# Expert weights split once and reloaded as parts, and a planner that orders the readers of a PSUM bank

## The chip, the cores and the metric

One of the cores of a Trainium2 chip runs the whole program. The metric is the device time of one execution in microseconds (us). Below, PE is TensorE, PEld its weight loads, DVE is VectorE, ACT is ScalarE, POOL is GpSimd, and SP is SyncE, whose queue issues most DMAs.

## The reference

Three layers follow each other, in fp32, on 8 batches of 3072 tokens of width 256:

```python
attn = np.maximum(z @ z.T / S, 0.0) ** 2       # per batch
x = u * (attn @ v)
# expert layer: tokens with x @ w_skip > 0 go to their argmax expert of 8
h = np.maximum(xc[mask] @ w1[e], 0.0)
y[mask] = gate_w[mask, None] * (h @ w2[e])      # x[do_compute] += y
# rational layer, on every token
h = x @ w_in
P = a[0] + a[1] * h + a[2] * h2 + a[3] * h3
Q = 1.0 + np.abs(b[0]) * np.abs(h) + np.abs(b[1]) * h2
out = (P / (Q + 1e-06)) @ w_out
```

## The kernel before

Every fp32 operand of a large matrix product is kept as two parts, hi (a rounded copy) and lo (the operand less hi), and a product takes three matmuls (hi hi, hi lo, lo hi) in PE's fp32r format. Splitting an operand of 128x512 costs one copy and one subtraction on ACT, DVE or POOL.

**Work units.** Attention goes in 1152 ticks (a 512 x 256 block of scores: matmuls, relu and square on ACT, split on ACT or DVE, product with V). The expert and the rational layer go in 1024 units of 256 tokens by 256 hidden columns; each unit has 12 matmuls into a PSUM bank h (L1030), elementwise work, and 12 matmuls into the accumulator bank accM (L1041), of which there is one. An expert unit needs ACT's relu (L1166, hi) and DVE's subtraction (L1169, lo). A rational unit, number t, needs, in order of its names in `plan_unit`: abs (ACT, L1174, reads h), p1 (ACT, L1175, reads h), q0 (ACT, POOL or DVE, L1181 or L1179), q1 (DVE or POOL, the L394 multiply mq<-mq,mu), p2 (DVE, L1187, reads h), p3 (DVE, L1188), ln and ex (ACT, L1189 and L1190), gh (DVE, L1191), v (DVE, L1192), w (DVE, L1194, the last reader of h, which frees the bank) and gl (POOL or DVE, the L394 multiply mgl<-mq,mu).

**Stages.** The batches form five groups of 1, 2, 2, 2 and 1. A group's tokens go through attention, are scattered to their experts, then through the expert units, then the rational units; attention ticks of the next group are mixed in between. In the profile: ticks alone to 366 us; the first group's 32 expert units to 464; its rational units with ticks to 1300; expert units of the second group to 1535, its rational units with ticks to 2720; the same for the third group (2720 to 2945 to 4085) and the fourth (4085 to 4310 to 5020, the last ticks in it). From 5020 to 5370 comes a **mixed stage** without attention: 56 rational units of group four and the 32 expert units of group five. The **last stage** (5370 to the end) is the 96 rational units of group five.

**Weights.** An expert has four chunks; a chunk is a 128x512 piece of w1 and one of w2. `plan_w1` loads a chunk's two pieces in fp32 (two DMAs of 256 KB on SP's queue into the ring wr), makes hi by two copies and lo by two subtractions, into a tile W of 128x2048 (a ring of eight). It does so for each of the four groups with an expert stage of their own and, with other buffers (Wr, Wv), for group five: 160 times for 32 different chunks. The rational layer's weights are converted and split once, at the start, stored in DRAM as wsc, and loaded as parts by POOL's queue (L973).

**What sets the order.** All instructions are placed by a list scheduler in the kernel itself (`Flow`). Each operation has a due time, shifted by a table of numbers (`PAR`), an estimate of its length on each engine that could do it, what it waits for, and buffers that it takes and frees. `Flow.run` fixes which engine does it and the order on each engine. Waits in the built program are put in by the framework from the tiles and banks that an instruction reads and writes, in that order; the engines run their queues strictly in order.

## Time and profile before

| | before |
|---|---|
| median of 3 runs (lowest to highest) | 5769.25 us (5768.03 to 5769.51) |
| profiled execution: time, span | 5767.14 us, 5765.4 us |
| granted TensorE clock, mean | 0.994 |
| busy: PE, DVE, ACT, POOL | 5498.1, 4701.9, 4315.3, 3309.7 us |
| DMA: moved, mean | 335.30 MB, 58 GB/s |

Busy time is the sum over the span, and it hides that stages differ: the table of stages in the rows below gives, for each stage, its length and each engine's busy time in it. PE's busy time less the stage's length is what PE waited there. The list of waits names, for one engine in one stretch, whose instruction ended each wait.

### The profile page before, as it was taken

Reading aid. Unit: us, or ns where it says so; the run is one execution under the profiler, and the core shown is the slowest. Engines: PE = TensorE matmul, PEld = TensorE weight load, DVE = VectorE, ACT = ScalarE, POOL = GpSimd, SP = SyncE. Lnnn points to the kernel's source line nnn. Section 1 sums busy time; section 2 is a strip of 40 time slices with the busy share of each in tenths; the row PEclk is TensorE's granted clock in tenths of the full one; section 3 lists DMA queues with packets and bytes.
Section 4 is the critical chain, followed back from the end, with each engine's and each line's share of the span. In section 5 each row is a group of like instructions: output and inputs, shape, how many; then the busy total and the mean of one; then the engine's idle time right before and its main releaser. Section 6 shows DMA issues by size and latency. Waiting matters only on the chain.

```text
span 5765.4 us, 119268 instructions
## 1 busy us (share of the span) xinstructions
PE 5498.1 (95%) x45285; PEld 5417.3 (94%) x45285; DVE 4701.9 (82%) x7546; ACT 4315.3 (75%) x7907; POOL 3309.7 (57%) x4614
## 2 busy tenths in 40 slices
PE   9999999999999999999999999999999999988887
PEld 8999999999999999999999999999999999887776
DVE  6766777776588888888568899889759999988999
ACT  7877787885488888888458888888638888755776
POOL 3443444445565665666455675567556666655677
PEclk9999999999999999999999999999999999999999
DMA  4353111023400100011330010001241000122000
GB/s 134 105 167 116 30 59 32 31 62 94 151 27 30 53 31 31 28 52 45 105 127 24 27 59 27 29 25 54 72 143 50 24 22 24 37 81 65 19 19 14
DMA packets 261771, 335.30 MB, mean 58 GB/s; under 512 B 31102, under 2 KB 211817, under 8 KB 256066
## 3 DMA queue, kind: packets, MB, share of 16 engines
q1 hardware_dynamic: 233922, 259.87, 14.6%
q0 software_dynamic: 27264, 67.71, 3.4%
q8 instruction: 358, 5.87, 0.4%
q14 instruction: 227, 1.86, 0.1%
HBM read 224.54 MB, written 119.54 MB: 60 GB/s over the span
## 4 chain that ended last, share of the span: by engine, by line
PE 59%; DVE 19%; ACT 8%; issue 6%; POOL 6%; DMA 1%; SPq 0%; DVEq 0%; POOLq 0%; ACTq 0%
PE accA L672 20%; PE h L1030 15%; PE accM L1041 14%; DVE mq L1192 4%; PE S L649 4%; PE S L650 3%; DVE mp L1187 3%; DVE mgh L1191 3%; DVE mq L1194 3%; ACT mu L1174 2%; POOL mq L394 2%; DVE h L1188 2%; ACT mp L1175 2%; DVE al L664 1%; ACT mu L1189 1%
## 5 line engine op out<-in xcount | busy, mean ns | idle before, releaser
L1030 PE MATMUL h<-mx,W 128*128 128x256 f32 x11904 | 1621.8, 284 | 136.1 <-DVE mq L1194 121.2
L1030 PEld LDWEIGHTS h<-mx,W 128*128 128x128 f32 x11904 | 1489.9, 190 | 167.3 <-DVE mq L1194 75.3
L672 PE MATMUL accA<-V,ah 128*128 128x256 f32 x9216 | 1295.1, 283 | 1.2 <-DVE ah L400 0.8
L394 POOL TENSOR_TENSOR mgl<-mq,mu 128x512 fp32r<-128x512 f32 x626 | 835.8, 1335 | 672.3 <-DVE mq L1194 392.4
L672 PEld LDWEIGHTS accA<-V,ah 128*128 128x128 f32 x9216 | 1181.2, 190 | 2.5 <-issue 0.9
L1041 PE MATMUL accM<-W,mgh 128*128 128x256 f32 x7936 | 1118.7, 284 | 28.1 <-ACT mo L1089 21.3
L1041 PEld LDWEIGHTS accM<-W,mgh 128*128 128x128 f32 x7936 | 1019.0, 190 | 34.9 <-ACT mo L1089 25.6
L664 DVE TENSOR_TENSOR al<-S,ah 128x512 fp32r<-128x512 f32 x1152 | 786.3, 683 | 165.5 <-ACT ah L398 158.3
L1175 ACT ACTIVATE mp<-h,coef 128x512 f32<-128x512 f32 x768 | 593.7, 773 | 258.3 <-PE h L1030 251.8
L1187 DVE TENSOR_TENSOR mp<-mp,h 128x512 f32<-128x512 f32 x768 | 523.4, 682 | 301.7 <-ACT mu L1174 197.0
L1181 POOL TENSOR_SCALAR mq<-mu,coef 128x512 f32<-128x512 f32 x494 | 399.2, 808 | 640.3 <-ACT mu L1174 609.2
L653 ACT ACTIVATE S<-S 128x512 f32<-128x512 f32 x1152 | 673.7, 590 | 104.2 <-PE S L650 99.4
L672 PE MATMUL accA<-V,al 128*128 128x256 f32 x4608 | 747.0, 284 | 2.2 <-DVE al L664 1.3
L1189 ACT ACTIVATE mu<-mq 128x512 f32<-128x512 f32 x768 | 484.4, 631 | 314.4 <-POOL mq L394 172.7
L656 ACT ACTIVATE S<-S 128x512 f32<-128x512 f32 x1152 | 669.1, 586 | 20.8
L1041 PE MATMUL accM<-W,mgl 128*128 128x256 f32 x3968 | 644.1, 284 | 28.2 <-POOL mgl L394 27.0
L1192 DVE SCALAR_TENSOR_TENSOR mq<-mq,mgh 128x512 f32<-128x512 f32 x768 | 646.1, 841 | 13.4 <-DVE mgh L1191 0.5
L394 POOL TENSOR_TENSOR mq<-mq,mu 128x512 f32<-128x512 f32 x431 | 599.4, 1391 | 90.2 <-ACT mq L1179 61.6
L672 PEld LDWEIGHTS accA<-V,al 128*128 128x128 f32 x4608 | 632.3, 191 | 5.2 <-DVE al L664 5.0
L1191 DVE SCALAR_TENSOR_TENSOR mgh<-h,coef,mu 128x512 fp32r<-128x512 f32 x768 | 570.8, 743 | 76.4 <-ACT mu L1190 73.4
L1188 DVE SCALAR_TENSOR_TENSOR h<-mp,coef,h 128x512 f32<-128x512 f32 x768 | 575.4, 749 | 46.5 <-ACT mu L1174 34.2
L398 ACT ACTIVATE ah<-S 128x512 fp32r<-128x512 f32 x954 | 566.2, 594 | 42.8 <-PE accA L672 35.8
(157 smaller groups left out, 8797.9 us busy)
## 6 DMA issues: line engine op xcount, KB each, us to landing
wr<-in_moe_w_dram SPq DMA_DIRECT2D x256, 256.0 KB, 3.3
W<-wsc POOLq DMA_DIRECT2D x32, 1024.0 KB, 6.6
vr<-in_v_dram SPq DMA_DIRECT2D x96, 256.0 KB, 3.1
xs<-in_u_dram SPq DMA_DIRECT2D x96, 256.0 KB, 2.8
x<-xs SPq DMA_DIRECT2D x96, 256.0 KB, 2.2
mr<-x SPq DMA_DIRECT2D x96, 256.0 KB, 3.3
out_dram<-mo SPq DMA_DIRECT2D x96, 256.0 KB, 2.1
xs<-dflt SPq DMA_DIRECT2D x128, 129.0 KB, 3.5
```

What stands on the lines that cost most here:

```text
L394: (nc.vector if e == "D" else nc.gpsimd).tensor_tensor(*a, **k)
L653: act(st["s"], st["s"], AF.Relu, scale=1.0 / S)
L656: act(st["s"], st["s"], AF.Square)
L664: ttt(st["lo"], st["s"], st["hi"].bitcast(F32), op=ALU.subtract)
L672: mm(accs[b, ic][:, it * TT : (it + 1) * TT], lhsT=a[:, jj * TT + it * P : jj * TT + (it + 1) * P], rhs=VV[b, jp][:, vi, jj * D : (jj + 1) ...
L1030: mm(o, lhsT=lw, rhs=rw, start=(ff == 0 and k == 0 and i == 0), stop=(ff == 1 and k == NK - 1 and i == 2), skip_group_check=True,)
L1041: mm(acc[:, it * TT : (it + 1) * TT], lhsT=(gh, gl)[part][:, c0 : c0 + P], rhs=w[i][:, 512 + ff * D : 512 + (ff + 1) * D], start=(first an ...
L1175: pt("p1", "A.664", ["l1b"], lambda: act(buf("mp"), s["h"], AF.Identity, scale=a3, bias=a2), ["mp"])
L1187: pt("p2", "D.602", ["p1"], lambda: ttt(s["p"], s["p"], s["h"], op=ALU.mult))
L1188: pt("p3", "D.663", ["p2", "abs"], lambda: stt(s["h"], s["p"], a1, s["h"], op0=ALU.add, op1=ALU.mult), (), ["mp"])
L1191: pt("gh", "D.663", ["ex", "p3"], lambda: stt(buf("mgh", F32R), s["h"], a0, s["u"], op0=ALU.add, op1=ALU.mult), ["mgh"])
L1192: pt("v", "D.602s", ["gh"], lambda: stt(s["q"], s["q"], CQ, s["gh"].bitcast(F32), op0=ALU.add, op1=ALU.mult))
```

## The change

1. `plan_w1` now splits only the first group's 32 chunks, and stores each W tile (hi and lo, 1 MB) to a DRAM tile wsc1 through SP's queue. The W buffer comes free only when the unit has used it and the store has read it.
2. `plan_w1_again` is new: the later 128 uses load the parts from wsc1 (one DMA of 1 MB, or two of 512 KB for group five), with no split.
3. The planner's rules: p2 comes after abs, so that DVE reads bank h after ACT has read it twice; a POOL instruction that waits for another engine is planned 0.1 us later; the count update r10 is planned after the previous row's r11.
4. The numbers: the table PAR and four entries of SLIP and AHEAD are others, so that the whole order differs. A line or two stands for the table.

```diff
-    "S.a": 1.49, "S.t": -1.49, "T1.a": 5.12, "T1.s": 6.55, "T1.t": -6.87, "T1hi.a": 1.51, "T1hi.s": -1.21,
+    "S.a": 4.71, "S.t": -3.11, "T1.a": -18.46, "T1.s": 5.48, "T1.t": -40.77, "T1hi.a": -69.55, "T1hi.s": -2.13,
...
-SLIP = {"P": 1.52, "A": 0.4, "D": 19.82, "G": 3.13, "Q": 9.0}
+SLIP = {"P": 3.38, "A": 0.24, "D": 3.82, "G": 19.29, "Q": 9.0}
...
-    AHEAD = {"P": 8.21, "A": 5.51, "D": 27.32, "G": 9.0, "Q": 0.0}
+    AHEAD = {"P": 10.61, "A": 4.39, "D": 83.31, "G": 9.23, "Q": 0.0}
...
-                t = max(t, f if e == pe == "P" else f + LAT[pe])
+                t = max(t, f if e == pe == "P" else f + LAT[pe] + (0.1 if e == "G" != pe else 0.0))
...
+    wsc1 = tc.dram_tile([E * FP1, P, 2048], F32R, name="wsc1")
...
-            (10, 10, "G.6", r10, (9,), old(10), [], []),
+            (10, 10, "G.6", r10, (9,), old(10, 11) + ([("ct", g - 1, 0)] if g and bl == 0 and ic == 1 else []), [], []),
...
+        def store():
+            nc.sync.dma_start(out=wsc1[c].bitcast(F32), in_=wt_t["tile", n].bitcast(F32))
...
+        add(xx + 2.0, ("wsc1", c), "Q.73", store, after=[("W", n)])
...
+    def plan_w1_again(n, c):
+
+        v = isinstance(n, tuple)
+
+        def load():
+            if v:
+                wt_t[n] = [sb.tile([P, 1024], F32R, tag="V", name=f"Wv{i}_{c}", bufs=NJP) for i in range(2)]
+                for i in range(2):
+                    nc.sync.dma_start(out=wt_t[n][i].bitcast(F32), in_=wsc1[c][:, 1024 * i : 1024 * i + 1024].bitcast(F32))
+            else:
+                wt_t[n] = whole(n)
+                nc.sync.dma_start(out=wt_t["tile", n].bitcast(F32), in_=wsc1[c].bitcast(F32))
+
+        flow.tag = "v" if v else "n"
+        add(
+            w_first[n][0] - 24.0, ("W", n), "Q.73 Q.73" if v else "Q.73", load, after=[("wsc1", c)],
+            takes=WV(n) if v else [("W", n)],
+        )
...
-            pt("p2", "D.602", ["p1"], lambda: ttt(s["p"], s["p"], s["h"], op=ALU.mult))
+            pt("p2", "D.602", ["p1", "abs"], lambda: ttt(s["p"], s["p"], s["h"], op=ALU.mult))
...
-            at["l2l"], ("l2l", t), "P.476", lambda: l2(1), after=[("gl", t), ("l2h", t)],
+            at["l2l"], ("l2l", t), "P.476", lambda: l2(1),
+            after=[("gl", t), ("l2h", t)] + ([("wsc1", wn)] if wn in range(E * FP1) and w_last[wn] == t else []),
```

Counted in the two built programs: the weight copies (128x512) go from 129 + 40 to 51 on ACT, from 59 + 12 to 8 on DVE and from 68 + 12 to 5 on POOL, the weight subtractions from 133 + 43 to 61 on DVE and from 123 + 21 to 3 on POOL (the second number of a pair is group five's). PE's instructions are the same, 47278. Which engine does the rational units' movable work also differs:

| stage | q1 on DVE | q1 on POOL | gl on DVE | q0 on ACT | q0 on POOL |
|---|---|---|---|---|---|
| 464 to 1300 | 81, now 53 | 7, now 35 | 20, now 30 | 14, now 6 | 55, now 75 |
| 1535 to 2720 | 80, now 94 | 112, now 98 | 47, now 44 | 49, now 50 | 143, now 140 |
| 2945 to 4085 | 80, now 68 | 112, now 124 | 47, now 40 | 56, now 41 | 136, now 137 |
| 4310 to 5020 | 43, now 21 | 101, now 123 | 27, now 17 | 61, now 26 | 83, now 109 |
| mixed stage | 28, now 23 | 28, now 33 | 1, now 3 | 27, now 11 | 29, now 45 |
| last stage | 25, now 0 | 71, now 96 | 0, now 0 | 48, now 60 | 48, now 36 |

Three places in the order of instructions follow. A number in a tile's name is that of its unit or chunk, and the second one is a running number. The first is DVE's order late in the mixed stage, around the expert units 909 to 912 and the rational units 910 and 911, before:

```order
L394 TENSOR_TENSOR Wv1_28_75428<-Wr_28_75126,Wv0_28_75427 128x512
L1169 SCALAR_TENSOR_TENSOR mgl909_75453<-h909_75301,mgh909_75446 128x512
L394 TENSOR_TENSOR Wv1_28_75428<-Wr_28_75126,Wv0_28_75427 128x512
L1070 TENSOR_TENSOR mx146_75451<-mt146_75382,mx146_75451 128x512
L400 CAST Wv0_29_75472<-Wr_29_75424 128x512
L1084 SCALAR_TENSOR_TENSOR mo144_75492<-accM144_75400,mr144_74991 128x256 x2
L1188 SCALAR_TENSOR_TENSOR h911_75352<-mp911_75389,coef_102,h911_75352 128x512
L394 TENSOR_TENSOR Wv1_29_75473<-Wr_29_75424,Wv0_29_75472 128x512
L394 TENSOR_TENSOR mq911_75502<-mq911_75502,mu911_75481 128x512
L400 CAST Wv0_30_75520<-Wr_30_75448 128x512
L1191 SCALAR_TENSOR_TENSOR mgh910_75540<-h910_75314,coef_102,mu910_75371 128x512
```

and in the change (its lines stand some 19 further down: L1188 is before's L1169, L1206 its L1187, L1207 its L1188, L1210 its L1191):

```order
L1188 SCALAR_TENSOR_TENSOR mgl909_74663<-h909_74532,mgh909_74657 128x512
L1206 TENSOR_TENSOR mp910_74669<-mp910_74669,h910_74545 128x512
L1089 TENSOR_TENSOR mx146_74671<-mt146_74566,mx146_74671 128x512
L1207 SCALAR_TENSOR_TENSOR h910_74545<-mp910_74669,coef_103,h910_74545 128x512
L1103 SCALAR_TENSOR_TENSOR mo144_74707<-accM144_74616,mr144_74139 128x256 x2
L1210 SCALAR_TENSOR_TENSOR mgh910_74719<-h910_74545,coef_103,mu910_74602 128x512
L1206 TENSOR_TENSOR mp911_74711<-mp911_74711,h911_74579 128x512
L1188 SCALAR_TENSOR_TENSOR mgl912_74743<-h912_74699,mgh912_74728 128x512
L1211 SCALAR_TENSOR_TENSOR mq910_74605<-mq910_74605,mgh910_74719 128x512
```

The copies and subtractions of Wv are gone from between the units' own work, and p2 and p3 of the units are what stands there. The second place is SP's queue of DMAs in the first group's expert stage, before:

```order
L349 DMA wr10_0_6017<-in_moe_w1_dram 128x2x256
L353 DMA wr10_1_6018<-in_moe_w2_dram 128x2x256
L349 DMA wr11_0_6094<-in_moe_w1_dram 128x2x256
L353 DMA wr11_1_6095<-in_moe_w2_dram 128x2x256
L349 DMA wr12_0_6136<-in_moe_w1_dram 128x2x256
L353 DMA wr12_1_6137<-in_moe_w2_dram 128x2x256
L750 DMA x2_1_73<-xs13_5582 128x2x256
```

and in the change:

```order
L956 DMA wsc1_70<-W7_5787 128x2048
L349 DMA wr10_0_5892<-in_moe_w1_dram 128x2x256
L353 DMA wr10_1_5893<-in_moe_w2_dram 128x2x256
L956 DMA wsc1_70<-W8_5867 128x2048
L349 DMA wr11_0_5957<-in_moe_w1_dram 128x2x256
L353 DMA wr11_1_5958<-in_moe_w2_dram 128x2x256
L956 DMA wsc1_70<-W9_5933 128x2048
L349 DMA wr12_0_6023<-in_moe_w1_dram 128x2x256
L353 DMA wr12_1_6024<-in_moe_w2_dram 128x2x256
```

A store of 1 MB stands between the loads of 256 KB each, and waits there until its chunk is split. The third place is DVE's order in the last stage, around unit 943, before:

```order
L1188 SCALAR_TENSOR_TENSOR h944_76838<-mp944_76875,coef_102,h944_76838 128x512
L1194 SCALAR_TENSOR_TENSOR mq942_76873<-h942_76733,coef_102,mq942_76873 128x512
L394 TENSOR_TENSOR mq944_76936<-mq944_76936,mu944_76925 128x512
L1187 TENSOR_TENSOR mp945_76944<-mp945_76944,h945_76878 128x512
L1191 SCALAR_TENSOR_TENSOR mgh943_76976<-h943_76795,coef_102,mu943_76906 128x512
L1187 TENSOR_TENSOR mp946_76966<-mp946_76966,h946_76899 128x512
L1188 SCALAR_TENSOR_TENSOR h945_76878<-mp945_76944,coef_102,h945_76878 128x512
L1192 SCALAR_TENSOR_TENSOR mq943_76918<-mq943_76918,mgh943_76976 128x512
L1191 SCALAR_TENSOR_TENSOR mgh944_77001<-h944_76838,coef_102,mu944_76925 128x512
L1194 SCALAR_TENSOR_TENSOR mq943_76918<-h943_76795,coef_102,mq943_76918 128x512
L1192 SCALAR_TENSOR_TENSOR mq944_76936<-mq944_76936,mgh944_77001 128x512
```

and in the change:

```order
L1206 TENSOR_TENSOR mp944_76074<-mp944_76074,h944_76030 128x512
L1210 SCALAR_TENSOR_TENSOR mgh943_76165<-h943_75971,coef_103,mu943_76107 128x512
L1207 SCALAR_TENSOR_TENSOR h944_76030<-mp944_76074,coef_103,h944_76030 128x512
L1211 SCALAR_TENSOR_TENSOR mq943_76117<-mq943_76117,mgh943_76165 128x512
L1210 SCALAR_TENSOR_TENSOR mgh944_76192<-h944_76030,coef_103,mu944_76124 128x512
L1213 SCALAR_TENSOR_TENSOR mq943_76117<-h943_75971,coef_103,mq943_76117 128x512
L1211 SCALAR_TENSOR_TENSOR mq944_76136<-mq944_76136,mgh944_76192 128x512
L1206 TENSOR_TENSOR mp945_76190<-mp945_76190,h945_76078 128x512
L1213 SCALAR_TENSOR_TENSOR mq944_76136<-h944_76030,coef_103,mq944_76136 128x512
```

The multiply q1 of unit 944 is no longer on DVE; it is on POOL, as all 96 of this stage are.

## Rows read from the trace of the kernel before

**Rows 1.** By stage: length, busy PE PEld DVE ACT POOL, PE clock, DMA share, GB/s.
```profile
...
366.00:464.00 98.00, 97.85 (x830) 97.56 (x829) 71.87 (x125) 50.20 (x92) 47.37 (x68) 1.00 0.64 199
...
1300.00:1535.00 235.00, 233.28 (x1964) 232.18 (x1964) 133.60 (x218) 107.08 (x198) 130.31 (x192) 1.00 0.36 112
1535.00:2720.00 1185.00, 1162.81 (x9695) 1150.28 (x9694) 1017.92 (x1648) 966.01 (x1798) 719.60 (x1029) 1.00 0.13 42
...
4310.00:5020.00 710.00, 669.43 (x5503) 657.18 (x5503) 661.03 (x1009) 572.26 (x1017) 444.98 (x517) 1.00 0.10 31
5020.00:5370.00 350.00, 285.11 (x2149) 276.49 (x2147) 303.32 (x425) 204.03 (x342) 202.73 (x191) 0.93 0.22 69
5370.00:5765.00 395.00, 307.03 (x2422) 292.20 (x2420) 381.89 (x540) 293.92 (x469) 297.56 (x226) 0.99 0.05 17
...
```

**Rows 2.** Waits of PE in the mixed stage: total, times, longest.
```profile
...
PE h L1030 <- DVE mq L1194: 24.1, 12, 4.3
PE accM L1041 <- POOL mgl L394: 15.9, 8, 4.1
...
PE h L1030 <- DVE Wv L394: 0.4, 1, 0.4
...
```

**Rows 3.** DVE by line in 5045 to 5333, inside the mixed stage.
```profile
...
L394 DVE TENSOR_TENSOR Wv<-Wr,Wv 128x512 fp32r<-128x512 f32 x40 | 34.1, 867 | 0.2
...
L394 DVE TENSOR_TENSOR mq<-mq,mu 128x512 f32<-128x512 f32 x24 | 30.0, 1251 | 7.0 <-POOL mq L1181 3.2 <-ACT mq L1179 2.5
...
L400 DVE CAST Wv<-Wr 128x512 fp32r<-128x512 f32 x12 | 8.0, 684 | 0.0
...
```

**Rows 4.** Waits of PE in the last stage.
```profile
...
PE h L1030 <- DVE mq L1194: 62.1, 49, 1.7
...
```

**Rows 5.** DVE by line in 5333 to 5765.
```profile
...
L1192 DVE SCALAR_TENSOR_TENSOR mq<-mq,mgh 128x512 f32<-128x512 f32 x106 | 99.1, 935 | 0.2
...
L394 DVE TENSOR_TENSOR mq<-mq,mu 128x512 f32<-128x512 f32 x27 | 33.2, 1230 | 2.6 <-POOL mq L1181 1.6 <-ACT mq L1179 1.0
...
```

**Rows 6.** POOL by line in 5333 to 5765.
```profile
...
L394 POOL TENSOR_TENSOR mgl<-mq,mu 128x512 fp32r<-128x512 f32 x107 | 157.2, 1470 | 41.2 <-PE accM L1041 19.8 <-DVE mq L1194 16.1 <-ACT mu L1189 2.2
L394 POOL TENSOR_TENSOR mq<-mq,mu 128x512 f32<-128x512 f32 x78 | 113.6, 1456 | 18.3 <-ACT mq L1179 14.0
L1181 POOL TENSOR_SCALAR mq<-mu,coef 128x512 f32<-128x512 f32 x53 | 42.6, 804 | 51.5 <-ACT mu L1174 51.5
...
```

**Rows 7.** Transposes of two neighbouring row tiles on PE, last stage (start, length).
```profile
...
5390.10 0.60 PE L1062 MATMUL mt<-ident_r,mr 128*128 128x128 f32 x4
...
5420.87 0.60 PE L1062 MATMUL mt<-ident_r,mr 128*128 128x128 f32 x4
...
```

**Rows 8.** DVE by line in 4324 to 5045, before the mixed stage.
```profile
...
L394 DVE TENSOR_TENSOR mq<-mq,mu 128x512 f32<-128x512 f32 x45 | 31.7, 704 | 0.4 <-POOL mq L1181 0.4
L394 DVE TENSOR_TENSOR mgl<-mq,mu 128x512 fp32r<-128x512 f32 x27 | 28.0, 1039 | 0.1
...
```

**Rows 9.** As rows 1, for the first expert stage and just behind it.
```profile
...
327.00:460.00 133.00, 132.82 (x1118) 132.11 (x1117) 94.33 (x167) 80.26 (x154) 64.05 (x117) 1.00 0.57 175
460.00:470.00 10.00, 10.00 (x86) 10.00 (x86) 2.94 (x5) 8.35 (x16) 1.82 (x3) 1.00 1.06 423
...
```

**Rows 10.** DMA issues: kilobytes each, median microseconds to landing.
```profile
...
W<-wsc POOLq DMA_DIRECT2D x32, 1024.0 KB, 6.6
...
```

**Rows 11.** Waits between ACT and DVE over the whole program.
```profile
...
DVE mp L1187 <- ACT mu L1174: 197.0, 216, 3.2
...
ACT mu L1174 <- DVE mp L1187: 102.4, 187, 4.0
...
```

**Rows 12.** DVE in 5370 to 5757: shortest, median and longest (ns).
```profile
...
L1192 DVE SCALAR_TENSOR_TENSOR mq<-mq,mgh x101: 677/745/1621, 5370.4 to 5753.2; 128x512 f32<-128x512 f32 x101
...
L394 DVE TENSOR_TENSOR mq<-mq,mu x25: 680/687/1777, 5383.1 to 5750.4; 128x512 f32<-128x512 f32 x25
...
```

**Rows 13.** POOL in 5370 to 5765: shortest, median and longest (ns).
```profile
...
L394 POOL TENSOR_TENSOR mq<-mq,mu x74: 1266/1304/1672, 5372.5 to 5745.5; 128x512 f32<-128x512 f32 x74
...
```

More of the change, by code (lines that the diff above doesn't have):

```diff
@@ L925, in plan_w @@
         for n, (kind, c) in enumerate(wlist):
-            if kind == "w1":
+            if kind == "w2":
+                plan_w2(n, c)
+            elif n < E * FP1:
                 plan_w1(n, c)
             else:
-                plan_w2(n, c)
+                plan_w1_again(n, c)
         if NG > 1:
             for c in range(E * FP1):
-                plan_w1(("v", c), c)
+                plan_w1_again(("v", c), c)
     def plan_w1(n, c):
         xx = w_first[n][0] - 15.0
-        v = isinstance(n, tuple)
-        tk, tr = (WV(n), [("V", ("raw", n))]) if v else ([("W", n)], [("wr", ("raw", n, i)) for i in range(2)])
+        tr = [("wr", ("raw", n, i)) for i in range(2)]
         def load():
-            if v:
-                r = sb.tile([P, 1024], F32, tag="V", name=f"Wr_{c}", bufs=NJP)
-                raw[n] = r[:, 0:512], r[:, 512:1024]
-            else:
-                raw[n] = [tl("wr", f"wr{n}_{i}") for i in range(2)]
+            raw[n] = [tl("wr", f"wr{n}_{i}") for i in range(2)]
             w_load(*raw[n], w1[c // FP1], w2[c // FP1], c % FP1)
@@ L949, in hi @@
             if half == 0:
-                if v:
-                    wt_t[n] = [sb.tile([P, 1024], F32R, tag="V", name=f"Wv{i}_{c}", bufs=NJP) for i in range(2)]
-                else:
-                    w = tl("W", f"W{n}", F32R, 2048)
-                    wt_t[n] = [w[:, 0:1024], w[:, 1024:2048]]
+                wt_t[n] = whole(n)
             o = 512 * half
@@ L960, in lo @@
             tt_on(e, w[1][:, o : o + 512], raw[n][half], w[0][:, o : o + 512].bitcast(F32), op=ALU.subtract)
-        flow.tag = "v" if v else "f" if c < FP1 else "n"
+        def store():
+            nc.sync.dma_start(out=wsc1[c].bitcast(F32), in_=wt_t["tile", n].bitcast(F32))
+        flow.tag = "f"
         add(xx - 5.0, ("Wl", n), "Q.73 Q.73", load, takes=tr)
-        add(xx, ("Wh", n, 0), "A.52|D.335s|G.588", lambda e: hi(e, 0), after=[("Wl", n)], takes=tk)
+        add(xx, ("Wh", n, 0), "A.52|D.335s|G.588", lambda e: hi(e, 0), after=[("Wl", n)], takes=[("W", n)])
@@ L965, in plan_w1 @@
         add(xx + 0.6, ("Wh", n, 1), "A.52|D.335s|G.588", lambda e: hi(e, 1), after=[("Wh", n, 0)])
-        add(xx + 0.8, ("Wo", n), "D.602s|G1.245t", lambda e: lo(e, 0), after=[("Wh", n, 0)], frees=[] if v else tr[:1])
-        add(xx + 1.4, ("W", n), "D.602s|G1.245t", lambda e: lo(e, 1), after=[("Wh", n, 1), ("Wo", n)], frees=tr if v else tr[1:])
+        add(xx + 0.8, ("Wo", n), "D.602s|G1.245t", lambda e: lo(e, 0), after=[("Wh", n, 0)], frees=tr[:1])
+        add(xx + 1.4, ("W", n), "D.602s|G1.245t", lambda e: lo(e, 1), after=[("Wh", n, 1), ("Wo", n)], frees=tr[1:])
@@ new lines, in plan_w1, with whole @@
+        add(xx + 2.0, ("wsc1", c), "Q.73", store, after=[("W", n)])
+    def whole(n):
+        w = wt_t["tile", n] = tl("W", f"W{n}", F32R, 2048)
+        return w[:, 0:1024], w[:, 1024:2048]
+    def plan_w1_again(n, c):
[6 more added lines that the diff above has]
+            else:
+                wt_t[n] = whole(n)
+                nc.sync.dma_start(out=wt_t["tile", n].bitcast(F32), in_=wsc1[c].bitcast(F32))
[4 more added lines that the diff above has]
+        )
@@ L969, in plan_w2 @@
     def plan_w2(n, fp):
         def load():
-            w = tl("W", f"W{n}", F32R, 2048)
-            wt_t[n] = [w[:, 0:1024], w[:, 1024:2048]]
-            nc.gpsimd.dma_start(out=w, in_=wsc[fp])
+            wt_t[n] = whole(n)
+            nc.gpsimd.dma_start(out=wt_t["tile", n], in_=wsc[fp])
         xx = w_first[n][0] - 30.0
```

22 lines of the change are left out of this document (9 added, 13 removed), and 35 rows, old and new, of the table PAR.

## The prediction

> **What bounds the kernel now.** The profile is read in this order: stages, then PE's waits in the stages where PE is not full, then the lines of the engine that PE waits for. The table of stages shows that PE is full nearly everywhere: in the expert stages it works 97.85 of 98 us and 233.3 of 235 us, in a rational stage with attention 1162.8 of 1185 us (22 us idle; the third group's is like it) [rows 1]. Only three stages leave much: 710 us with 40.6 us idle, the mixed stage's 350 us with 64.9, and the last stage's 395 us with 88 [rows 1]. A gain must come from these; what ACT, DVE or POOL save elsewhere is hidden behind a full PE. In these three DVE is the busiest of the helpers: 661 of 710 us, 303 of 350 and 382 of 395 [rows 1]. In the last stage PE's wait is 62.1 us for line L1194, the last reader of a bank h [rows 4]. In the mixed stage the same wait leads with 24.1 us, and the next is POOL's gl with 15.9 [rows 2]. TensorE's granted clock is 0.93 in the mixed stage, and about 1 in the others [rows 1].
>
> **The change, part by part.**
>
> *Splits in the expert stages of groups two to four.* 96 chunks lose two copies and two subtractions each. PE works 233.3 of 235 us in such a stage [rows 1], so this is worth nothing by itself; the cover is PE's own work, and 1.7 us per stage is all that could come back.
>
> *Splits in the mixed stage.* DVE loses 34.1 us of subtractions and 8.0 us of copies [rows 3], and five of 28 q1 by the count, 5 x 1.25 = 6.3 us [rows 3]: 48.4 us of its 303.3, leaving 254.9. If DVE stays as busy as now, 303.3/350 = 87%, the stage takes 254.9/0.867 = 294 us, 56 less. Bounds: PE is named as waiting for DVE's Wv itself for 0.4 us only [rows 2], which gives 0 if the work is only filler; and PE's idle 64.9 us plus what the lower clock costs, 0.07 x 285 = 20 us [rows 1], gives 85. I take 50, nearer to the DVE sum because DVE's wait leads the list [rows 2], a little under it because the waits for POOL's gl stay.
>
> *Multiplies moved from DVE to POOL, last stage.* All 25 q1 on DVE go, 25 x 1.230 = 30.8 us [rows 5], of a DVE that works 382 of 395 us [rows 1]. POOL gains 25 x 1.456 = 36.4 us and loses 12 q0 of 0.804 us, 9.6 us [rows 6]: 297.6 + 26.8 = 324 us, still under DVE's 351. A tile of eight units takes 30.8 us now [rows 7]; 30.8 us saved over twelve tiles would make it 28.2. Bounds 0 and 31. I take 20, since POOL, at 324 of 375 us, will now be late at times: gl ends a unit and gives back its buffer.
>
> *The same in the stage 4310 to 5020.* DVE loses 22 q1 of 0.704 us and 10 gl of 1.039 us [rows 8], 25.9 us of 661. At an unchanged share (93%) the stage shortens by 28 us; bounds 0 and the 40.6 us that PE idles [rows 1]. I take 20.
>
> *The two long rational stages* get 14 more and 12 fewer q1 on DVE. PE has 22 us idle in each [rows 1]. Zero, with 20 us either way.
>
> *Stores in the first expert stage.* 32 stores of 1 MB (1.05 million bytes) join its loads. At saturation the queues moved 423 GB/s with 1 MB transfers [rows 9], so a store takes 2.48 us and 32 take 79 us. From 327 to 460 us the DMA engines were 57% busy [rows 9], so 57 of 133 us are free: the stores are 22 us over. The last eight (20 us) can run after the last load, so about 2 us are exposed, plus loads landing later; I take +8. Bounds: 0, and stores no faster than this stretch's loads, 175/0.57 = 307 GB/s [rows 9], 3.4 us each: 109 us, 52 over. The Trainium skill's page DMA: Bandwidth & Descriptors (list of terms at its head) puts the limit of one core's HBM traffic at about 358 GB/s; by it, as an estimate, 32 stores take 94 us, 37 over. The 10 us at 423 GB/s speak against that as a hard limit here, but for loads only. In SP's order a store waits for its split, and behind it stand loads three chunks on, whose wr buffers the next splits must free anyway: the wait queues nothing that could start. That W comes free only after the store is inside the bounds.
>
> *Loads of parts later.* 32 x 2.48 = 79 us of DMA in each stage of about 235 us [rows 1, 9]. One landed in 6.6 us from POOL's queue [rows 10]; the plan asks for them 10.9 of its microseconds ahead (24.0 less W.n's 13.1). Zero, up to 6.6 us late once per stage: 0 to +20.
>
> *Bank order.* DVE already waits for abs 216 times and abs for p2 187 times [rows 11]. p2 and abs share only the bank h, so the built program already lets one engine at a time at it. The new rule takes away no collision and adds no wait; it fixes who goes first, ACT. Priced within the stages above. POOL's 0.1 us and r10's dependency move plan times only: zero, hidden as before.
>
> **Sum.** -50 - 20 - 20 + 8 = -82 us on the profiled 5767.1 us, 5685; the median of the three runs is 2.1 us above the profiled one, so 5687 us.
>
> **Rivals.**
>
> 1. *The split work was filler.* One accumulator bank and three buffers for a unit's chain set the mixed stage, and DVE's freed time turns into idle time. For it: Wv is named for 0.4 us, gl for 15.9 [rows 2]. Against it: DVE's 87%. The mixed stage then gives 10 us, the sum is -42: 5727 us.
> 2. *POOL's multiplies block DVE.* DVE's v and q1 take 0.68 us at the shortest but 1.62 and 1.78 at the longest [rows 12], and POOL's multiply 1.27 to 1.67 [rows 13]: in the last stage each lengthens the other. Moving 25 q1 from 0.68 us on DVE to 1.27 on POOL adds 14.8 us to the time in which one of them holds the other up, so the last stage gains nothing: -62, 5707 us. SBUF — State Buffer in the Trainium skill (Who interferes with whom) says that a DVE instruction with two SBUF inputs and a GpSimd instruction that reads SBUF exclude each other, the later one blocking fully, which speaks against this move; the longest rows agree, the medians of 0.745 and 1.304 us show that it is not the rule.
> 3. *The stores are slow* and the first expert stage pays the 52 us: 5687 + 44 = 5731 us.
> 4. *Slower: DVE now waits where ACT waited.* 187 times p2 went first and abs waited, 102.4 us in all, 0.55 each [rows 11]. With abs always first these waits go to DVE's queue, where gh, v and w of older units, and so the banks, stand behind them. If all 102 us lie on the path, the sum is +20: 5789 us. It decides from 80% of them (82/102). Against it: ACT idles there too, and in the mixed and last stages little of DVE's idle time could be spent so.
> 5. *Nothing arrives.* PE's waits stay what they are and only stores are added: 5769 + 8 = 5777 us.
>
> **How the numbers follow.** Forecast 0.55, rivals 0.17, 0.10, 0.10, 0.05 and 0.03. The range 5640 to 5745 us holds the forecast with its good side (the mixed stage at 85 us and the last at 31 would make it 5641) and rivals 1 to 3; it leaves out rivals 4 and 5, and sums of several bad bounds. About 0.2% (11.5 us) is what a measurement tells from no change. Faster by more: 0.90 (the forecast and rivals 1 to 3, less a little for two of them together); within: 0.03; slower: 0.07.
>
> **What would show it.** Right: the mixed stage near 300 us with PE's wait for L1194 well under 24 us; no q1 on DVE in the last stage, the distance of its transposes from 30.8 us to about 29.1; PE idle in the 710 us stage near 20 us; PE in the first expert stage 0 to 20 us idle, waiting for W. Wrong: the mixed stage still over 335 us (rival 1); v's mean over 1.0 us in the last stage and its tiles still at 30.8 (rival 2); PE waiting 40 us or more for W at 370 to 500 us (rival 3); DVE's waits for abs grown by 80 us or more and rational stages longer (rival 4). A gain beyond 130 us would mean that the long rational stages gave something, which I put at zero.

## The result and the profile after

The changed kernel takes 5641.73 us (median of 6 runs, 5639.19 to 5643.04), the kernel before, measured beside it, 5768.03 (5 runs); the ratio is 0.9781, with an interval of 0.9768 to 0.9794. A sixth execution of the kernel before took 9484.39 us and is left out. The forecast was 5687 us, 82 below; the gain is 126. It lies inside the range by 1.7 us, and 4 us short of what the prediction had tied to a cause it did not believe in: "A gain beyond 130 us would mean that the long rational stages gave something, which I put at zero."

The head of the profile after, busy us by engine:

```profile
span 5641.3 us, 118833 instructions
...
PE 5436.9 (96%) x45285; PEld 5385.1 (95%) x45285; DVE 4527.7 (80%) x7338; ACT 4221.9 (75%) x7703; POOL 3183.5 (56%) x4514
...
```

PE issues the same 45285 matmuls that it issued before, yet its busy time fell by 61 us, from 5498.1, at the same mean clock (0.994 and 0.993). Busy time is not a fixed amount of work here.

**Where the time went.** Stage borders shift, so both traces are cut at the same program points: PE's transposes of attention rows (tile xp, 96 rows, counted from 0), the first transposes of the last stage (5390.10 before, [rows 7], and 5275.45 after), and the end. In us:

| stretch | before | after | difference | forecast |
|---|---|---|---|---|
| start to row 13: attention ticks | 372.3 | 376.1 | +3.8 | 0 |
| rows 13 to 14: first expert stage | 118.3 | 154.8 | +36.5 | +8 |
| 14 to 36: rational, group one | 817.8 | 794.1 | -23.7 | 0 |
| 36 to 39: around the expert stage of group two | 302.1 | 296.1 | -6.0 | 0 |
| 39 to 62: rational, group two | 1144.1 | 1112.1 | -32.0 | 0 |
| 62 to 64: expert stage, group three | 265.2 | 266.4 | +1.2 | 0 |
| 64 to 85: rational, group three | 1094.4 | 1064.9 | -29.5 | 0 |
| 85 to 87: expert stage, group four | 287.6 | 283.7 | -3.9 | with the next |
| 87 to 95: rational, group four | 627.7 | 608.6 | -19.1 | -20 |
| row 95 to the last stage: mixed | 360.7 | 318.7 | -42.0 | -50 |
| last stage | 375.3 | 365.9 | -9.4 | -20 |
| sum (spans 5765.4, 5641.3) | | | -124.1 | -82 |

The work between two borders is not quite the same in both programs: the counts of matmuls below (after an x) differ by up to 17 in the long stages and by 38 in rows 87 to 95, which at 0.12 us each is 2 and 5 us.

So the total came near by luck, through misses of opposite sign: the first expert stage lost 28 us more than forecast, and the three long rational stages gave 85 us that were priced at zero.

The table of stages, first expert stage and the long rational stages of groups one to three, between the program points of the table, before (columns as in [rows 1]):

```profile
372.26:490.58 118.32, 118.17 (x999) 117.93 (x998) 76.98 (x131) 70.31 (x129) 45.99 (x68) 1.00 0.66 218
490.58:1308.37 817.79, 809.92 (x6655) 794.83 (x6654) 610.24 (x1060) 662.60 (x1274) 371.50 (x722) 1.00 0.14 41
...
1610.43:2754.49 1144.06, 1119.83 (x9320) 1107.37 (x9318) 994.90 (x1610) 940.67 (x1753) 703.70 (x1010) 1.00 0.12 37
3019.73:4114.17 1094.44, 1071.28 (x8881) 1058.71 (x8881) 978.65 (x1561) 912.28 (x1679) 689.95 (x954) 1.00 0.12 36
...
```

and after, with the mixed and the last stage as the last two lines:

```profile
376.06:530.85 154.79, 131.15 (x1016) 128.95 (x1015) 75.59 (x131) 74.86 (x140) 44.43 (x78) 0.92 0.82 307
530.85:1324.98 794.13, 790.08 (x6638) 786.79 (x6636) 614.96 (x1055) 648.05 (x1231) 402.92 (x754) 1.00 0.15 47
...
1621.10:2733.21 1112.11, 1103.71 (x9308) 1099.29 (x9307) 993.42 (x1629) 932.39 (x1744) 665.37 (x985) 1.00 0.13 41
2999.62:4064.51 1064.89, 1053.16 (x8864) 1047.24 (x8863) 962.23 (x1552) 905.17 (x1670) 686.85 (x954) 1.00 0.12 39
...
4956.78:5275.45 318.67, 279.32 (x2219) 271.94 (x2220) 263.92 (x379) 179.72 (x297) 182.92 (x183) 0.96 0.36 128
5275.45:5641.00 365.55, 297.29 (x2330) 279.17 (x2328) 350.02 (x498) 295.29 (x464) 301.74 (x229) 0.99 0.06 18
...
```

In the stage of group two PE left 24.2 us idle before (1144.06 less 1119.83) and the stage became 32 us shorter: more than all of PE's idle time. The rest came out of its busy time, 16 us less for the same matmuls. The weight loads (PEld) leave 36.7 us before and 12.8 after, and the gain lies inside that. The Trainium skill, Perfetto Trace Analysis (Identifying the Most-Contended Engine), says that matmul busy time is a poor measure of how near a kernel is to its limit because matmuls are pipelined, and names the busy share of weight loads as one of two to use instead; the trace agrees for groups two and three (36.7 us hold the 32, 35.7 the 29.5). A bound it is not: in group one the weight loads left 23.0 us idle and the stage gave 23.7.

The start times of the single matmuls in the traces show where it comes from. Successive matmuls start 119 to 120 ns apart in the median of these stages, before and after, while one matmul counts as busy for some 280 ns. A pause shorter than that stays hidden in the busy time. What the distances over 130 ns exceed 120 by sums to 35.7, 49.2 and 51.1 us in the stages of groups one, two and three before, and to 15.6, 22.4 and 26.9 after: 20, 27 and 24 us less, for gains of 23.7, 32 and 29.5, of which 1.4 to 2 us each are matmuls that moved across the borders. PE was not as full as its 1162.8 of 1185 us [rows 1] made it look.

The waits between engines over the whole program, before, for the two lines that [rows 11] doesn't show:

```profile
ACT mu L1189 <- POOL mq L394: 172.7, 238, 3.4
...
PE h L1030 <- DVE mq L1194: 122.3, 106, 4.3
...
```

and after (L1206 is p2, L1193 abs, L1208 ln, L1213 w):

```profile
ACT mu L1208 <- POOL mq L394: 117.1, 172, 2.8
...
DVE mp L1206 <- ACT mu L1193: 242.7, 248, 3.9
...
PE h L1049 <- DVE mq L1213: 49.6, 75, 1.4
...
```

ACT's 102.4 us of waiting for p2 [rows 11] are no longer among its waits. DVE's waits for abs grew by 46 us. ACT's wait for the q1 of POOL fell, and PE's wait for the last reader of a bank h is less than half.

### The profile page after: what moved, and what is told of

The parts are those of the page before. It is cut to its first block, busy times and chain, and to the rows that moved or that the text cites. A ratio compares the mean times of both kernels' runs of the same rounds, so it can differ in the third digit from the quotient of the medians.

```text
span 5641.3 us, 118833 instructions
## 1 busy us (share of the span) xinstructions
PE 5436.9 (96%) x45285; PEld 5385.1 (95%) x45285; DVE 4527.7 (80%) x7338; ACT 4221.9 (75%) x7703; POOL 3183.5 (56%) x4514
## 4 chain that ended last, share of the span: by engine, by line
PE 73%; DVE 14%; issue 4%; DMA 3%; ACT 3%; POOL 2%; SPq 0%; DVEq 0%; POOLq 0%; ACTq 0%
PE accA L672 25%; PE h L1049 18%; PE accM L1060 18%; PE S L649 4%; PE S L650 4%; DVE mq L1211 4%; DVE mgh L1210 2%; DVE mp L1206 2%; DVE h L1207 2%; DVE mq L1213 2%; DMA wr<-in_moe_w_dram 1%; PE lp L761 1%; DVE al L664 1%; PE mt L1081 1%; POOL mgl L394 1%
## 5 line engine op out<-in xcount | busy, mean ns | idle before, releaser
L1049 PE MATMUL h<-mx,W 128*128 128x256 f32 x11904 | 1661.4, 283 | 74.8 <-DVE mq L1213 49.6
L1049 PEld LDWEIGHTS h<-mx,W 128*128 128x128 f32 x11904 | 1508.6, 190 | 97.8 <-issue 31.9
L1060 PE MATMUL accM<-W,mgh 128*128 128x256 f32 x7936 | 1098.7, 282 | 30.8 <-ACT mgh L1185 14.1
L1060 PEld LDWEIGHTS accM<-W,mgh 128*128 128x128 f32 x7936 | 1003.8, 190 | 36.4 <-ACT mgh L1185 16.8
L1200 POOL TENSOR_SCALAR mq<-mu,coef 128x512 f32<-128x512 f32 x542 | 447.2, 825 | 527.0 <-ACT mu L1193 467.8
L1206 DVE TENSOR_TENSOR mp<-mp,h 128x512 f32<-128x512 f32 x768 | 523.6, 682 | 257.6 <-ACT mu L1193 242.7
L394 POOL TENSOR_TENSOR mq<-mq,mu 128x512 f32<-128x512 f32 x509 | 676.7, 1331 | 63.4 <-ACT mq L1198 30.1
L1211 DVE SCALAR_TENSOR_TENSOR mq<-mq,mgh 128x512 f32<-128x512 f32 x768 | 688.6, 897 | 15.0 <-POOL mgl L394 0.5
L1210 DVE SCALAR_TENSOR_TENSOR mgh<-h,coef,mu 128x512 fp32r<-128x512 f32 x768 | 571.4, 744 | 59.3 <-ACT mu L1209 53.6
L650 PE MATMUL S<-T,T 128*128 128x256 f32 x2304 | 600.0, 284 | 0.0
L398 ACT ACTIVATE ah<-S 128x512 fp32r<-128x512 f32 x924 | 548.5, 594 | 65.4 <-PE accA L672 59.6
L1208 ACT ACTIVATE mu<-mq 128x512 f32<-128x512 f32 x768 | 484.3, 631 | 150.8 <-POOL mq L394 117.1
```

The lines of the kernel that those rows point to most:

```text
L394: (nc.vector if e == "D" else nc.gpsimd).tensor_tensor(*a, **k)
L650: mm(o, lhsT=lw, rhs=T4[b, ic], start=False, stop=(jj == 1), skip_group_check=True)
L1049: mm(o, lhsT=lw, rhs=rw, start=(ff == 0 and k == 0 and i == 0), stop=(ff == 1 and k == NK - 1 and i == 2), skip_group_check=True,)
L1060: mm(acc[:, it * TT : (it + 1) * TT], lhsT=(gh, gl)[part][:, c0 : c0 + P], rhs=w[i][:, 512 + ff * D : 512 + (ff + 1) * D], start=(first an ...
L1206: pt("p2", "D.602", ["p1", "abs"], lambda: ttt(s["p"], s["p"], s["h"], op=ALU.mult))
L1210: pt("gh", "D.663", ["ex", "p3"], lambda: stt(buf("mgh", F32R), s["h"], a0, s["u"], op0=ALU.add, op1=ALU.mult), ["mgh"])
```

## The experiments

Every kernel is cut at the same program points; "tail" is row 95 to the end. Where the number of runs is not given it was one; the four or five runs of the others lie 2 to 16 us apart, so single differences of less than some 15 us are not told from none.

### Which edit shortened the rational stages

The theory after the result: the bank rule (p2 after abs) did it. The rival: the other table of numbers did.

Bank rule taken out of the changed kernel:

```diff
-            pt("p2", "D.602", ["p1", "abs"], ...
+            pt("p2", "D.602", ["p1"], ...
```

> The changed kernel with p2 no longer planned after abs; nothing else is changed. Theory C (the bank rule gives the gain of the long rational stages): they lose 40 us or more of 96, 5680 us or above, and ACT again waits for p2 of DVE. Theory A (the numbers give it): within 20 us of 5642. The numbers were found with the rule in force, so some loss would not speak for C by itself; the place of it would.

5676.5 us, 35 slower, 4 us short of what the theory asked for. The first three rational stages lose 12, 20 and 16 us, some half of their gain, as the theory said; the fourth gains 23, the tail loses 10. ACT's wait for p2 is back, but small, since the new table sends p2 late:

```profile
ACT mu L1193 <- DVE mp L1206: 18.3, 17, 1.8
...
```

The same rule put into the kernel before, and nothing else:

```diff
-            pt("p2", "D.602", ["p1"], ...
+            pt("p2", "D.602", ["p1", "abs"], ...
```

> The kernel before with one edit: p2 is planned after abs. Theory C' (of the 93 us gained in the long rational stages about 48 are the bank rule's, as the run without it showed): 5715 to 5730 us, the gain in the three long stages, 12 to 20 us each, and ACT's waits for p2 gone. Rival (the rule helps only together with the other edits): within 15 us of 5767, or slower.

5649.75 us, 120 below the 5769.7 of the kernel before beside it, far more than the 5715 to 5730 expected: nearly the whole gain of the change, without a single weight reloaded. The rational stages shorten by 21, 25, 31 and 56 us, the tail grows by 16. The table of stages, rational stages of groups two and four and the tail:

```profile
1588.75:2707.83 1119.08, 1108.87 (x9321) 1103.85 (x9319) 998.72 (x1598) 942.93 (x1773) 704.09 (x1004) 1.00 0.12 38
...
4323.96:4896.10 572.14, 570.47 (x4803) 568.09 (x4801) 564.21 (x915) 510.37 (x923) 377.29 (x448) 1.00 0.09 27
4896.10:5648.00 751.90, 608.92 (x4527) 580.38 (x4527) 703.70 (x987) 483.50 (x795) 443.23 (x385) 0.93 0.13 41
...
```

and its waits:

```profile
ACT mu L1189 <- POOL mq L394: 79.6, 120, 3.3
...
DVE mp L1187 <- ACT mu L1174: 218.7, 233, 3.0
...
PE h L1030 <- DVE mq L1194: 88.5, 83, 2.6
...
```

That the edit does it is shown, in both directions. How it does it, the rows show in part. In both programs the readers of a bank h go one at a time, since ACT waited for p2 and DVE for abs before [rows 11]. The plan of before did not know it. It let DVE's p2 go as soon as p1 was there, so abs, the first step of the chain abs, q0, q1, ln, ex, gh, v, w, stood behind p2, and ACT, in order, stood still with it. With the rule abs goes first; p2 is needed only at gh, so it can wait. DVE's waits for abs grow by 22 us, ACT's 102.4 us vanish, and q1 is there earlier for ln (172.7 to 79.6 us of waiting for POOL's q1). The Trainium skill, PSUM — Partial Sum Buffer (PSUM bank collisions raise a hardware error), wants two engines kept apart by bank; the 187 and 216 waits of [rows 11] agree that the built program did so before the change too.

This chain fits the stage of group four, where 37.2 of the 102.4 us lie (gain 56). It does not fit all of the gain: groups one, two and three hold 0.4, 18.3 and 12.2 us of them and gained 21, 25 and 31; without the rule in the changed kernel 18.3 us of these waits are back and the three stages lose 48. In group one other waits fell with the rule. The waits of that stage, before:

```profile
DVE mp L1187 <- ACT mu L1174: 136.3, 78, 3.2
ACT mu L1189 <- DVE mq L394: 38.8, 62, 1.5
...
ACT mu L1174 <- DVE mp L1187: 0.4, 1, 0.4
...
```

and with the bank rule in the kernel before:

```profile
DVE mp L1187 <- ACT mu L1174: 110.1, 74, 3.0
...
ACT mu L1189 <- DVE mq L394: 8.1, 14, 1.0
...
```

Here it was DVE that stood at p2, for an abs that the plan did not make it wait for, and its q1 came late for ln. The rule moves the whole order, since the planner places everything around p2 anew; no run separates this from the wait itself.

The other rule alone (a POOL instruction that waits for another engine is planned 0.1 us later), and both rules together, each in the kernel before:

```diff
-                t = max(t, f if e == pe == "P" else f + LAT[pe])
+                t = max(t, f if e == pe == "P" else f + LAT[pe] + (0.1 if e == "G" != pe else 0.0))
...
```

> The kernel before with one edit: the plan counts 0.1 us more for a POOL instruction that waits for another engine. Theory E (the other 45 us of the long stages, which neither numbers, nor splits, nor the bank rule account for, are this rule's): 5715 to 5735 us, 10 to 15 us in each long stage. Rival (they are another edit's, the count update's place or the absent split work): within 10 us of 5767.

5740.62 us, 29 below: the stages of groups two, three and four shorten by 18, 8 and 10 us, that of group one does not.

> The kernel before with both of the planner's rules (p2 after abs, and a POOL instruction that waits for another engine planned 0.1 us later), nothing else. Alone the first took 118 us off, the second 28. If they mend different waits: 5623 us, below the changed kernel without any part reloaded. If both mend the same chain (ACT's and POOL's lateness on the way to ln): 5645 to 5655 us, as the first alone. Where the tail stays at about 740 to 750 us, as with either rule alone, the split work keeps its worth in the tail.

5633.74 us (4 runs, 5632.59 to 5634.16; ratio 0.9768, 0.9751 to 0.9784): 16 below the bank rule alone, between the two expectations. The waits that they mend overlap in part. The tail is 732.1 us, about as before (736.0) and a little under the 740 to 750 expected. This version has no part reloaded, the old table, and is 8 us faster than the changed kernel in the medians; the intervals of the two ratios overlap.

### What the split, and what the table of numbers is worth

The changed kernel with the table, SLIP and AHEAD of before:

```diff
...
-SLIP = {"P": 3.38, "A": 0.24, "D": 3.82, "G": 19.29, "Q": 9.0}
+SLIP = {"P": 1.52, "A": 0.4, "D": 19.82, "G": 3.13, "Q": 9.0}
...
```

> The changed kernel (5641.7 us) with the table of numbers, SLIP and AHEAD of the kernel before; code, split weights and planner rules stay as changed. Theory A (the 96 us gained in the three long rational stages come from the new order that the numbers make): the long stages go back to their old pace, about 5735 us, the mixed stage still near 320 us. Theory B (they come from the splits that are gone): the long stages stay fast, 5650 to 5670 us. Theory C (they come from the rule that p2 follows abs): as B, long stages fast.

5648.87 us, 7 slower, which a single run does not tell from none. The three long rational stages take 794.6, 1113.3 and 1059.7 us, as fast as in the changed kernel: the table did not shorten them, and the rival falls. The numbers trade places elsewhere: with the old ones rows 87 to 95 are 16 us shorter and the tail is 33 us longer.

This kernel and the one with both rules have one table (but for the due times of the loads and splits); between them lies the split once with its stores and loads (and r10's dependency). The table of stages, first expert stage, mixed and last stage, for both rules without the split:

```profile
368.00:488.00 120.00, 119.29 (x1004) 118.53 (x1003) 76.30 (x130) 74.69 (x138) 41.69 (x66) 1.00 0.65 215
4898.87:5257.90 359.03, 297.28 (x2243) 287.57 (x2244) 332.54 (x461) 205.69 (x347) 206.11 (x199) 0.93 0.21 67
5257.90:5631.00 373.10, 309.26 (x2294) 294.56 (x2292) 352.93 (x543) 267.32 (x439) 238.08 (x190) 0.93 0.05 17
...
```

and with it:

```profile
370.42:523.37 152.95, 129.44 (x1006) 126.79 (x1004) 76.77 (x132) 72.38 (x131) 42.01 (x67) 0.93 0.90 342
4929.51:5271.40 341.89, 291.35 (x2244) 283.27 (x2245) 277.86 (x400) 179.25 (x303) 171.23 (x176) 0.95 0.35 120
5271.40:5647.00 375.60, 309.88 (x2294) 295.07 (x2292) 353.08 (x543) 267.55 (x439) 238.44 (x190) 0.93 0.06 17
...
```

DVE loses 54.7 us of work in the mixed stage (332.54 to 277.86), and the stage 17.1 us. The first expert stage grows by 33 us. In the median times the split costs 15 us (5633.74 to 5648.87, the second a single run). The gain of the change is then, edit by edit: rules -134, split +15, numbers -7, from 5768.0 to 5641.7. Only the first of the three is well clear of the spread of runs.

Three more kernels take splits away or bring them back in part. The chunks of groups two to four split at each use, as before, in the changed kernel:

```diff
             else:
-                plan_w1_again(n, c)
+                plan_w1_v(n, c)
...
+    def plan_w1_v(n, c):
...
```

> The changed kernel, but the chunks of groups two to four are loaded in fp32 and split again as before, with the old due times for these; group five still loads parts. Theory A: PE is full in those expert stages and the long stages keep their gain, 5640 to 5655 us. Theory B (the splits of the expert stages held up the rational stages beside them): 40 us or more lost, 5685 us or above.

5645.15 us, 3 slower, which is none: PE is full there, and the work was hidden, as the prediction had it. The same for group five:

```diff
-                plan_w1_again(("v", c), c)
+                plan_w1_v(("v", c), c)
...
```

> The changed kernel, but the 32 chunks of group five are loaded in fp32 and split again in the mixed stage; groups two to four load parts. Theory A (the mixed stage got its 42 us from DVE's 48 us of taken splits): the mixed stage is back at 350 to 360 us between the last row of attention and the second tile of the last stage, 5680 us or so. Rival (the mixed stage is faster by its order alone): less than 15 us lost, below 5657 us.

5721.7 us, 80 slower, 78 of it in the tail, and twice what was expected. The due times of this work are those of the old table, among units placed by the new one, so this is no clean price. The reverse, in the kernel before: group four's chunks stored, group five loads them as parts:

```diff
-                plan_w1(("v", c), c)
+                plan_w1_again(("v", c), c)
...
```

> The kernel before with one part of the change: group four's chunks are split as before and also stored, in an expert stage with free DMA time, and group five loads the parts; numbers and rules are those of before but for one due time. Theory A: the mixed stage gives 20 to 50 us, all else unchanged, 5717 to 5747 us. Rival (the work was filler there): less than 10 us, above 5757 us.

5802.53 us, 33 slower: the tail gains 2 us, and rows 85 to 87, where the stores were put, lose 37. SP's queue stood at these stores until their chunks were split:

```profile
SPq L976 <- DVE W L395: 42.8, 11, 9.2
...
```

Depending on the order around it, the same work saved in the tail gave 2, 15 or 78 us.

### What the stores cost

In the changed kernel's first expert stage the weight loads land late. DMA issues of 366 to 560, kilobytes each, median us to landing, after:

```profile
wsc<-W SPq DMA_DIRECT2D x27, 1024.0 KB, 8.9
wr<-in_moe_w_dram SPq DMA_DIRECT2D x46, 256.0 KB, 7.2
...
```

and before:

```profile
wr<-in_moe_w_dram SPq DMA_DIRECT2D x52, 256.0 KB, 3.6
...
```

The DMA engines were 0.95 busy at 356 GB/s for 110 us of it:

```profile
376.00:486.00 110.00, 91.15 (x699) 89.20 (x698) 56.30 (x100) 43.65 (x81) 34.86 (x66) 0.92 0.95 356
...
```

PE's clock was 0.92 there, and its busy time for some 1000 matmuls rose from 118.2 to 131.2 us; the other 23 of the 36 us are idle. None of this idle time is named for W. The rows point to ACT, which copies the loaded pieces and, behind them in its order, makes the hi of expert units (mgh). In the first expert stage before:

```profile
ACT W L398 <- DMA wr<-in_moe_w_dram: 4.8, 7, 1.3
...
```

and after, with PE's longest wait and with what SP's queue waited at the stores (L956):

```profile
ACT W L398 <- DMA wr<-in_moe_w_dram: 30.2, 14, 5.7
...
PE accM L1060 <- ACT mgh L1185: 10.2, 4, 5.5
...
SPq L956 <- DVE W L394: 6.4, 2, 4.6
...
SPq L956 <- POOL W L394: 4.1, 1, 4.1
...
```

Two theories: bytes, or SP's queue, where a store that waits for its split holds the loads behind it. The stores sent through POOL's queue:

```diff
-            nc.sync.dma_start(out=wsc1[c].bitcast(F32), in_=wt_t["tile", n].bitcast(F32))
+            nc.gpsimd.dma_start(out=wsc1[c].bitcast(F32), in_=wt_t["tile", n].bitcast(F32))
...
-        add(xx + 2.0, ("wsc1", c), "Q.73", store, after=[("W", n)])
+        add(xx + 2.0, ("wsc1", c), "G1.038 Q2.9", store, after=[("W", n)])
```

> The change with one edit: the 32 stores of parts are issued from POOL's queue instead of SP's. From the transposes of attention row 13 to those of row 14 the changed kernel takes 154.8 us, the kernel before 118.3. Theory A (order of a queue): the stores cost 36 us because each waits on SP's queue for its split and holds the loads behind it. Then this stretch falls to 120 to 135 us, and the time to 5610 to 5625 us. Theory B (bytes): the DMA engines were 95% busy there, and whose queue issues a store makes no difference. Then the stretch stays at 148 to 160 us, the DMA share near 0.95, and the time is 5630 to 5655 us. In either, POOL works some 30 us more, about 1 us per issue.

5654.14 us (4 runs; ratio 0.9801, 0.9785 to 0.9817), 12 slower, and the stage takes 170.9 us, above both expectations. With the stores gone from SP's queue the loads land in 5.7 us instead of 7.2, still not in 3.6, and POOL's queue now waits for the splits (an issue from it took 0.57 us in the median, not the 1 us expected):

```profile
wsc<-W POOLq DMA_DIRECT2D x27, 1024.0 KB, 8.2
wr<-in_moe_w_dram SPq DMA_DIRECT2D x50, 256.0 KB, 5.7
...
POOL wsc L956 <- DVE W L394: 38.1, 13, 6.8
...
```

So this run does not clear SP's order by itself, since it brought a wait of its own. What speaks against that order is the changed kernel, where SP stood 10.5 us at the stores in all. That the bytes are the whole cost is not shown: the DMA share fell to 0.80 over this longer stretch.

Next, stores spread in the program. Half of the chunks stored in the first stage, half in that of group two (`parts` says where a chunk is still split, `stores` where it is stored):

```diff
...
-            elif n < E * FP1:
+            elif n in parts:
...
+        if stores[c] == n:
+            add(xx + 2.0, ("wsc1", c), "Q.73", store, after=[("W", n)])
...
```

> The changed kernel, but only the 16 even chunks are stored in the first expert stage; the 16 odd ones are loaded in fp32, split and stored once more in group two's expert stage, where PE is full and the stage is longer; from group three on all are loaded as parts. Theory D (the first expert stage lost 36 us because stores and loads together exceed what the DMA engines move there): 16 stores take 40 us of 57 free, the stage loses 0 to 10 us instead of 36, 5610 to 5620 us in all. Rival (the loss is a matter of order, SP's queue or the splits' place, not of bytes): the stage stays 30 us or more over before, 5640 us.

5636.59 us (4 runs, 5627.41 to 5643.8; ratio 0.9770, 0.9753 to 0.9788), not told from the changed kernel and between its two expectations: rows 13 to 14 lose 16 us against the kernel before instead of 36 (22 in the next run, with the same stores), rows 36 to 39 lose 8 against the changed kernel. On top of it, the bank rule dropped for the rational units of group four only, where its absence had gained:

```diff
-            pt("p2", "D.602", ["p1", "abs"], ...
+            pt("p2", "D.602", ["p1"] + (["abs"] if not (kd == "x" and 704 <= t < 896) else []), ...
```

> The version with stores over two groups (5636.6 us) with one more edit: p2 is not planned after abs in the rational units of group four that stand among attention ticks. Rows 87 to 95 took 608.6 us there, 585.1 where the rule was left out everywhere. If that is the rule's own effect in this stretch, it becomes 580 to 590 us and the rest stays: about 5613 us. If it only comes from how the units before it were placed, the stretch stays at 600 to 612 or what it gains is paid back behind row 95 (694.7 us without the rule, 686.6 with it): 5630 to 5645 us.

5612.48 us (4 runs, 5609.49 to 5618.83; ratio 0.9729, 0.9713 to 0.9745): rows 87 to 95 take 589.4 us, the tail 688.1, as the first theory said. With the new table the rule hurts this stretch; with the old one it gained 56 us there. It is an ordering that fits or does not, not a law. Last, on this version, 16 stores in group two's stage and 16 in group three's, none in the first:

```diff
...
+        if kind_ == "w1":
+            k_ = seen[c_] = seen.get(c_, -1) + 1
+            if k_ <= 1 + c_ % 2:
+                parts[n_] = c_
+                stores[c_] = n_
...
```

> x10 (5612.5 us) with the stores moved once more: none in the first expert stage, 16 in that of group two and 16 in that of group three; a chunk is split until its store. What a store costs is then read a third time. If it costs 1 us in the first stage and 0.5 us in a stage of twice the length (16 stores took 16 us there and 8 here), rows 13 to 14 fall from 139.9 to about 119 us, rows 36 to 39 stay at 303, rows 62 to 64 go from 266 to 274: about 5600 us. If the cost goes with the number of stores alone, about 1 us each wherever they are, 5612 us as before.

**5594.94 us** (5 runs, 5590.16 to 5600.07; ratio 0.9699, 0.9686 to 0.9713), faster than both kernels and near the 5600 of its first theory. The table of stages, rows 13 to 14, 36 to 39 and 62 to 64:

```profile
368.58:490.56 121.98, 119.94 (x1016) 119.33 (x1015) 75.70 (x132) 75.39 (x142) 44.17 (x76) 1.00 0.51 162
1285.10:1583.45 298.35, 296.14 (x2509) 294.97 (x2509) 182.41 (x306) 165.83 (x304) 116.63 (x178) 1.00 0.50 172
2696.19:2971.39 275.20, 267.53 (x2249) 266.10 (x2249) 131.17 (x223) 116.01 (x210) 116.32 (x164) 0.99 0.56 198
...
```

Beside the changed kernel's 154.8, 296.1 and 266.4 us, 32 stores now cost about 11 us (2 and 9) where they cost 36. They were cheap here, sixteen at a time, with the DMA engines 0.50 and 0.56 busy in stages of 298 and 275 us. A long stage alone is not enough: all 32 in the stage of rows 85 to 87 cost 37 us (287.6 to 324.8), with the DMA engines 0.54 busy there.

## Why the prediction was right in the total and wrong in its parts

- **"The two long rational stages ... Zero": the step that failed.** They gave 32 and 29.5 us, group one's stage 23.7. PE's "22 us idle" was taken as all that could come back, and what the helpers save there as "hidden behind a full PE". But the pauses between PE's matmuls, most of them hidden in its busy time, were 49 and 51 us, and about half of them came back.
- **Bank order, "Priced within the stages above": wrong, and the cause of the first.** It was seen that the built program already ran the readers one at a time, and that the rule "adds no wait; it fixes who goes first". But who goes first was held to be neutral. Put into the kernel before, this edit alone is worth 120 us. Rival 4 had its sign reversed: DVE's waits for abs did grow, by 46 us, well under its 80, and PE did not pay for them.
- **POOL's 0.1 us, "zero, hidden as before": wrong too.** Alone it took 29 us off the kernel before (a single run), beside the bank rule 16.
- **Mixed stage, -50: measured -42, but in part for another reason.** DVE's saved work was well counted (48.4 us; 54.7 at one table). "If DVE stays as busy as now" failed: at one table the stage shortened by 17.1 us and DVE's share fell from 93 to 81%. So rival 1, that much of it was filler, holds for this part. The numbers add 23 (341.9 to 318.7), the rules 2; how the numbers do it is not shown. PE's waits after, in 4956 to 5250, first the one that [rows 2] has second, then its first:

```profile
PE accM L1060 <- POOL mgl L394: 11.0, 7, 4.6
...
PE h L1049 <- DVE mq L1213: 1.7, 3, 0.9
...
```

- **Last stage, -20: measured -9.4.** The distance of its transposes fell from 30.8 to 29.6 us, not to 29.1. It is the numbers' work: with the old ones the stage takes 375.6. All q1 are on POOL, as forecast, but v (L1211) became longer. DVE and POOL in the last stage, shortest, median and longest ns:

```profile
L1211 DVE SCALAR_TENSOR_TENSOR mq<-mq,mgh x97: 675/906/1631, 5275.9 to 5630.4; 128x512 f32<-128x512 f32 x97
...
L394 POOL TENSOR_TENSOR mq<-mq,mu x96: 1267/1296/1623, 5275.3 to 5625.6; 128x512 f32<-128x512 f32 x96
...
```

  v's median went from 745 [rows 12] to 906 ns, its mean from 935 [rows 5] to 1000, some 6 us over 97 of them. So half of rival 2 came true: POOL's multiplies lengthen DVE's two-input work, and take part of the gain. The single records show it: the 34 v that met no POOL multiply took 682 ns in the median, the 8 in which one began 685, and the 55 that began while one ran 1305. A POOL multiply that began under a v took 1670 ns in the median, one in which a v began 1285. Whichever began first held the other up. The prediction took the median of 745 ns as a sign that "it is not the rule"; that median mixes the two sorts (48 of 95 began under a multiply before). PE still waits here, less than in [rows 4]:

```profile
PE h L1049 <- DVE mq L1213: 42.5, 64, 1.2
...
```

- **Stage 4310 to 5020, -20: measured -19.1 and -3.9.** The size was right; that it came from fewer q1 and gl on DVE is not shown. The bank rule moves this stretch by -56 at the old table and +19 at the new one, and the old numbers shorten it by 16.
- **First expert stage, +8: mis-sized, +36.5**, inside its bounds of 0 to 52. The sum took free DMA time as usable at 423 GB/s and only an overhang as exposed; loads, stores and scatters together ran at 356 GB/s over 110 us, each load landed twice as late, and ACT stood 30 us for loads instead of 5. The 423 GB/s was read from a row whose DMA share is 1.06 [rows 9]; at a share of one it is 399, and the stores are 27 us over instead of 22. The Trainium skill, DMA: Bandwidth & Descriptors (Specifications), names a limit of about 358 GB/s; the estimate of 37 us made with it lies near the 36.5, and its rate near the 356 GB/s of this stretch, though 2.8 us slices of it ran at up to 435 GB/s. That the time agrees is in part luck: 13 of the 36.5 us are PE's longer busy time, which the estimate does not hold.
- **Splits of groups two to four, zero; later loads, zero:** right (3 us when put back; rows 36 to 39, 62 to 64 and 85 to 87 together -8.7).
- **Rivals 3 and 5:** 36.5 of rival 3's 52 us came, in a sum whose other terms covered it, but without its sign, a PE that waits 40 us or more for W: no wait of PE there names W. Rival 5 did not occur.

Open: why the same saved work in the tail is worth 2 to 78 us. It depends on the order of the rest, and no run here separates the two.
